# One core, forward and gradients of a two-branch block: the transpose of P by two DMAs of 16 blocks instead of one of 32, and a new order of all engines

## The chip, the cores and the metric

The kernel runs on one core of one Trainium2 chip. The metric is the device time of one execution in microseconds; lower is better. The kernel before took 1228.71 us in the median of three runs (1227.66 to 1231.55). One further execution was recorded with the hardware profiler; all rows of a profile in this document come from such a recorded execution, and their times count from its start.

A core has engines that run side by side, each through its own list of instructions in a fixed order: TensorE (PE, with its weight loads listed as PEld), VectorE (DVE), ScalarE (ACT), GpSimd (POOL) and SyncE (SP), which here issues transfers. An instruction waits, at the head of its list, until what it reads has been written and what it overwrites has been read. A transfer issued by SP is carried out by the DMA engines and lands later.

## The reference, cut to what matters

The reference is a block with two branches, run forward and then differentiated for a given `grad_out`. There are nine outputs: the block's output and the gradients of x and of seven weights. B = 2, T = 4000, D = 144, all bf16.

```
def _fwd_reference(x, w_qkv, w_att_out, w_mlp_in, dw_csgu, w_mlp_out, dw_merge, w_merge):
    xa = _layernorm(x, axis=-1)
    qkv = jnp.einsum('btd,de->bte', xa, w_qkv)
    ...
    scores = jnp.einsum('btd,bsd->bts', q, k) * D ** (-0.5)
    p = _softmax(scores, axis=-1)
    attn = jnp.einsum('bts,bsd->btd', p, v)
    glob = jnp.einsum('btd,de->bte', attn, w_att_out)
    ...
    loc = jnp.einsum('btd,de->bte', u * gc, w_mlp_out)
    m = jnp.concatenate([glob, loc], axis=-1)
    ...
    return x + jnp.einsum('btc,cd->btd', m, w_merge)

    _out, _vjp = jax.vjp(_f, x, w_qkv, w_att_out, w_mlp_in, dw_csgu, w_mlp_out, dw_merge, w_merge)
    _grads = _vjp(grad_out)
```

Most of the work is attention over 4000 positions and its gradient, which needs the 4000 x 4000 matrix of each batch several times.

## The kernel before, in words

The two batches follow each other. `phase_att` handles one batch in 32 tiles of 125 query positions (`PB`); a row of the score matrix is 32 blocks of 125 columns, stored 128 apart (4096 per row). A tile passes through several steps of one loop over `t`, so that a step works on several tiles at once:

- `products(q)`, q = 0 to 3: TensorE computes a chunk of 1000 columns of the scores S of tile t, and of dP (the gradient of the probabilities) of tile t−1. One chunk is four products of 500 columns and four remainders (L1059, L1065), called Q4 below.
- `S_min` (VectorE, L1083, L1085) copies a chunk of S into the buffer of P with the row minimum, `P_exp` (ScalarE, L1091) makes the exponentials in place, chunk by chunk in the order 1, 0, 3, 2.
- `P_tr` (L1095) transposes the whole row of P, 32 blocks, by one DMA that SP issues, from the buffer `Pb` into the one buffer `PT` (a part of `SX`). There are four buffers of P, three of S, and one `PT`.
- `Y_half` (L1115) reads `PT` in two halves of 16 products each and accumulates Y = P times the normalised x (with a column of ones for the row sum) in `yz`; called Y16 or Y32. VectorE then takes the reciprocal of the row sum (L1122) and the delta of the softmax gradient, ScalarE writes `yn` and `ty` (L1129, L1132), GpSimd the scaled rows that X needs (L1140 to L1144).
- `PdP` makes dS = dP times P: ScalarE casts a chunk of dP (L1104) and VectorE multiplies (L1106), or VectorE does both at once (L1101). `st_half` (L1287) transposes dS by two DMAs of 16 blocks each, and `Z_half` (L1162) multiplies them in two halves, called Z16. `zt_tr` (L1176) and the transposes of `qt` (L1041) and of `dhT` (L674) are further, smaller DMAs of the same queue.
- `X_group` (L1207) accumulates the gradient for the keys and values from untransposed P and dS; VectorE adds it up (L1213). The local branch is cut into small pieces that stand between these (L552 to L709).

Ahead of the loop stands a head: weights are multiplied together (L196 to L322), the first tiles of x are normalised and transposed (L459, L464), and 126 products that feed nothing (`WARM`, L154) keep TensorE running while data come in. Behind each batch come the weight gradients, the output and dx (L1487 to L1646), for the first batch beside the start of the second. In the very last tile of a batch the transposes are made on TensorE (`last_tr`, L1152), so 31 tiles of each batch use `P_tr`: 62 in all.

The order of every engine's instructions is written out by hand in the table `ORDER`: for each engine a list of numbers, each the difference to the one before, that name groups of instructions in the program's own order. `Planner.plan` turns the list into dependencies between neighbours, so an engine follows it exactly. What stands in the program decides only which data an instruction needs, and which numbers it has.

Of the kernel before, what the change touches and what calls it, by code (L numbers as in the profile page):

```python
# [747 lines left out]
for _s in """  # L748
PE 10 1 1 1 1 1 1 1 1 1 1 1 1 1 1 1 1 1 1 1 1 1 1 1 1 1 1 1 1 1 1 1 1 1 1 1 1 1 1 1 1 1 1 1 1 1 1 1 1 1 1 1 1 1 1 1 1 1 1 1 1 1 1 1 1 1 1 1 1 1 1 1 1
# [217 lines left out]
def phase_att(k, W, b, S, A, M, head=None, late=None, extra=None):  # L967
# [6 lines left out]
    with ExitStack() as es:  # L974
# [118 lines left out]
        def P_tr(i):  # L1093
            PL.tag("pt")
            nc.sync.dma_start_transpose(out=PT[:], in_=Pbuf[:, i % NPB, :])  # L1095
# [168 lines left out]
        for t in range(NB + 1):  # L1264
# [36 lines left out]
            if head is not None and t < 2:  # L1301
# [17 lines left out]
                if t == 0:  # L1319
                    P_tr(0)  # L1320
# [15 lines left out]
            pe(*((1,) if t < NB else range(4)))  # L1336
            products(0)
            pe(*((0,) if t < NB else ()))
            outs(2)
            if ok(t - 3):  # L1340
                zt_tr(t - 3)
            loc(0.25)
# [765 lines left out]
```

## Time and profile before

| | before |
|---|---|
| median of 3 runs | 1228.71 us |
| profiled execution, its own time | 1229.65 us |
| its span | 1227.9 us |
| mean granted TensorE clock | 0.996 |
| TensorE busy | 1183.7 us |
| VectorE busy | 1048.0 us |
| ScalarE busy | 734.7 us |
| GpSimd busy | 442.0 us |
| DMA queue of the transposes (q1), share of 16 engines | 86.4% |

A row of a group or of the timeline gives start, busy time, engine, line, operation, written and read tiles and, in brackets, how long the engine had been idle before it and for what. Engines ending in q (SPq) are the sequencers that issue transfers; the time of such a row is that of issuing. A row of a window gives from:to, its length, the busy time of PE, PEld, DVE, ACT and POOL, the granted clock, the DMA engines' mean busy share and GB/s. A row of the waits gives engine, line, what it waited for, us in total, times, and the longest. The rows themselves are shown in the prediction.

### The profile page before, as it was taken

To read this page: it belongs to the slowest core of one execution; us is meant where nothing else is said; L and a number is where in the kernel's file an instruction comes from. 1 tells how busy PE (TensorE), PEld (TensorE's weight loads), DVE (VectorE), ACT (ScalarE), POOL (GpSimd) and SP (SyncE) were. 2 spreads that over 40 slices of the span, in tenths; PEclk is the share of its full clock that TensorE was granted. 3 is DMA by queue.
4 is the path that set the end of the run, shared out by engine and by line. 5 is a ranking of instruction groups with operands and counts; after the bars stand their busy time and mean duration, and the time that the engine had idled before them with its cause. 6 is when DMAs were issued, how large, how long until landed. Compare 5 with 4: busy or idle time off the path is not lost.

```text
span 1227.9 us, 38426 instructions
## 1 busy us (share of the span) xinstructions
PE 1183.7 (96%) x15619; PEld 929.9 (76%) x15619; DVE 1048.0 (85%) x2856; ACT 734.7 (60%) x1303; POOL 442.0 (36%) x910
## 2 busy tenths in 40 slices
PE   9899999999999999998899999999999999998998
PEld 7567777777777777778777777777777777776987
DVE  7688989898989898878579998989898889996775
ACT  5866666666666666545747656666656565564461
POOL 8444334343443442314124433343433333332100
PEclk9999999999999999999899999999999999999999
DMA  3589899989999999997949899999899989999892
GB/s 107 111 147 159 149 175 161 166 148 166 164 149 169 154 166 169 150 200 147 180 102 167 157 161 169 163 165 164 141 172 160 171 155 168 162 163 173 161 167 69
DMA packets 681980, 191.81 MB, mean 156 GB/s; under 512 B 670572, under 2 KB 677481, under 8 KB 681796
## 3 DMA queue, kind: packets, MB, share of 16 engines
q1 hardware_dynamic: 656278, 181.97, 86.4%
q10 hardware_dynamic: 25348, 7.13, 3.0%
q8 instruction: 122, 2.00, 0.7%
q14 instruction: 56, 0.46, 0.1%
q0 software_dynamic: 176, 0.25, 0.1%
HBM read 20.44 MB, written 14.47 MB: 28 GB/s over the span
## 4 chain that ended last, share of the span: by engine, by line
PE 30%; DVE 11%; DMA 4%; ACT 2%; POOL 2%; issue 2%; SPq 1%; DVEq 0%; POOLq 0%; ACTq 0%
PE X L1207 7%; PE ps L1059 6%; PE yz L1115 3%; PE po L1609 3%; PE yz L1162 3%; DVE Pb L1083 3%; PE ps L1065 2%; DMA out_dram<-Pb 1%; DMA SX<-Pb 1%; DVE acc L1213 1%; DMA SX<-SX 1%; DVE SX L1101 1%; DVE SX L1106 1%; ACT Pb L1091 1%; PE po L1611 1%
## 5 line engine op out<-in xcount | busy, mean ns | idle before, releaser
L1091 ACT ACTIVATE Pb<-Pb,nm 125x1000 bf16<-125x1000 bf16 x256 | 273.7, 1124 | 127.0 <-DVE nm L1085 122.4
L1083 DVE TENSOR_SCALAR_CACHE_REDUCE Pb<-ps 125x1000 bf16<-125x1000 f32 x256 | 306.1, 1196 | 50.6 <-PE ps L1065 48.7
L1207 PE MATMUL X<-SX 125*128 125x144 bf16 x2048 | 293.0, 227 | 3.1 <-DVE acc L1213 1.7
L1207 PE MATMUL X<-SX,Pb 125*128 125x144 bf16 x2048 | 291.4, 226 | 2.8 <-DVE SX L1138 1.3
L1104 ACT CAST SX<-ps 125x1000 bf16<-125x1000 f32 x189 | 188.3, 996 | 142.3 <-PE ps L1065 136.7
L1059 PE MATMUL ps<-xaT_m,qt 128*128 128x500 bf16 x1024 | 261.3, 374 | 7.3 <-DVE Pb L1083 5.8
L1207 PEld LDWEIGHTS <-SX 125*128 125x128 bf16 x2048 | 197.3, 97 | 31.6 <-issue 31.0
L1213 DVE TENSOR_TENSOR acc<-X,acc 125x432 f32<-125x432 f32 (+1 forms) x372 | 199.4, 549 | 9.4 <-PE X L1207 8.8
L1207 PEld LDWEIGHTS <-Pb 125*128 125x128 bf16 x2048 | 200.2, 98 | 5.1 <-issue 4.1
L1162 PE MATMUL yz<-xa_aug,SX 125*128 125x144 bf16 x2048 | 149.7, 228 | 3.8 <-DMA SX<-SX 2.8
L1115 PE MATMUL yz<-xa_aug,SX 125*128 125x145 bf16 x2048 | 144.6, 228 | 5.7 <-DMA SX<-Pb 5.6
L1059 PEld LDWEIGHTS <-qt 128*128 128x128 bf16 x1024 | 91.8, 97 | 70.6 <-issue 12.3
L1106 DVE TENSOR_TENSOR SX<-SX,Pb 125x1024 bf16<-125x1024 bf16 x189 | 132.1, 702 | 9.1 <-ACT SX L1104 8.9
L1115 PEld LDWEIGHTS <-SX 125*128 125x128 bf16 x2048 | 133.6, 98 | 7.3 <-DMA SX<-Pb 7.0
L1162 PEld LDWEIGHTS <-SX 125*128 125x128 bf16 x2048 | 132.9, 98 | 8.1 <-DMA SX<-SX 4.3
L1065 PEld LDWEIGHTS <-qt 16*128 16x128 bf16 x1024 | 26.4, 91 | 109.7 <-issue 109.7
L1065 PE MATMUL ps<-XR,qt 16*128 16x500 bf16 x1024 | 102.7, 380 | 0.0
L1101 DVE TENSOR_TENSOR SX<-ps,Pb 125x1000 bf16<-125x1000 f32 x67 | 79.9, 1193 | 1.1 <-PE ps L1065 1.1
L557 POOL TENSOR_SCALAR l_a<-l_sq 125x576 bf16<-125x576 bf16 x32 | 23.3, 727 | 130.0 <-ACT l_sq L555 129.5
L1142 POOL TENSOR_SCALAR g<-qz,rl 125x144 f32<-125x144 bf16 x62 | 24.3, 393 | 116.3 <-DVE rl L1122 110.0
L662 POOL TENSOR_SCALAR l_w<-gdr,nc,c 125x144 f32<-125x144 bf16 x64 | 33.9, 534 | 59.7 <-DVE nc L658 32.5
L1487 PE MATMUL Hps<-Yg,go_h 125*128 125x144 bf16 x640 | 51.5, 228 | 0.3 <-DMA Yg<-Yn_d 0.3
(608 smaller groups left out, 2085.6 us busy)
## 6 DMA issues: line engine op xcount, KB each, us to landing
go_h<-in_grad_out_dram SPq DMA_DIRECT2D x4, 567.0 KB
Zn_d<-qz ACTq DMA_DIRECT2D x64, 35.2 KB
Yn_d<-yn ACTq DMA_DIRECT2D x64, 35.2 KB
ug_d<-ugr ACTq DMA_DIRECT2D x32, 70.3 KB
SX<-in_x_dram SPq DMA_DIRECT2D x16, 140.6 KB
out_dram<-Pb SPq DMA_DIRECT2D x16, 140.6 KB
out_dram<-SX SPq DMA_DIRECT2D x16, 140.6 KB
Pb<-in_grad_out_dram SPq DMA_DIRECT2D x8, 252.0 KB
```

The lines of the kernel that those rows point to most:

```text
L1059: mm = nc.tensor.matmul(pp[r // 2][:, r % 2, 0:CH], QT[i][:, 3 * h, :], xaTm[:, c * CH:(c + 1) * CH], start=True, stop=False)
L1065: nc.tensor.matmul(pp[r // 2][:, r % 2, 0:CH], QT[i][rs, 1 + h, :], xr, start=False, stop=True)
L1083: nc.vector.tensor_scalar(pv(Pbuf, i % NPB, c2), src, -1.0, 3.0e38, op0=ALU.mult, op1=ALU.min, accum_out=NM[i][:, c2:c2 + 1])
L1091: nc.scalar.activation(v, v, ACT.Exp, bias=NM[i][:, 4:5], scale=-1.0)
L1101: nc.vector.tensor_tensor(pv(Sbuf, i % NDB, c2), src, pv(Pbuf, i % NPB, c2), op=ALU.mult)
L1104: nc.scalar.copy(pv(Sbuf, i % NDB, c2), src)
L1106: nc.vector.tensor_tensor(sc, sc, pchunk(i % NPB, c2), op=ALU.mult)
L1115: nc.tensor.matmul(Y, PT[0:PB, j, :], xaa[:, j, 0:D + 1], start=(j == 0), stop=(j == NB - 1))
L1162: nc.tensor.matmul(Z, ST[0:PB, j, :], xaa[:, j, 0:D], start=(j == 0), stop=(j == NB - 1))
L1207: nc.tensor.matmul(X[:, jj, :], l, r, start=(n_ == 0), stop=(n_ == len(ops) - 1))
L1213: nc.vector.tensor_tensor(av, X[0:PB, 0:nj, :], av, op=ALU.add)
L1487: nc.tensor.matmul(H[a // 6][0:rows, a // 3 % 2, (a % 3) * D:(a % 3 + 1) * D], lhs, self.src[h][:, j, :], start=(j == 0 and a % 3 == 0), s ...
```

## The change

`P_tr` gets a second argument: half h of `PT` is transposed by a DMA of its own with 16 blocks. The first half (columns of chunks 0 and 1) is issued in the program right after the exponentials of chunks 1 and 0; the second half stands where the whole stood, after those of chunks 3 and 2. The first tile of a batch issues both halves together. No instruction is otherwise added or removed; the number of transposes of P rises from 62 to 124. The table `ORDER` is wholly new, for every engine (two of its rows are shown, cut).

```diff
 ORDER = {}
 for _s in """
-PE 10 1 1 1 1 1 1 1 1 1 1 1 1 1 1 1 1 1 1 1 1 1 1 1 1 1 1 1 1 1 1 1 1 1 1 1 1 1 1 1 1 1 1 1 1 1 1 1 1 1 1 1 1 1 1 1 1 1 1 1 1 1 1 1 1 1 1 1 1 1 1 1 1
...
+ 1 1 1 1 1 1 1 1 1 1 1 1 1 1 1 1 1 1 1 1 1 1 1 1 1 1 1 1 1 1 1 1 1 1 1 1 115 -114 117 -116 1 1 1 1 115 2 14 -130 1 1 1 1 1 1 149 2 -150 1 1 1 1 1 1
...
-        def P_tr(i):
-            PL.tag("pt")
-            nc.sync.dma_start_transpose(out=PT[:], in_=Pbuf[:, i % NPB, :])
+        def P_tr(i, h):
+            PL.tag("pt" if h else "pu")
+            a, w = h * NB // 2, NB // 2
+            nc.sync.dma_start_transpose(out=PT[:, a:a + w, :], in_=Pbuf[:, i % NPB, a * 128:(a + w) * 128])
...
                 if t == 0:
-                    P_tr(0)
+                    P_tr(0, 0)
+                    P_tr(0, 1)
                 continue
...
             products(0)
             pe(*((0,) if t < NB else ()))
+            if t < NB and ok(t - 1):
+                P_tr(t - 1, 0)
             outs(2)
...
             products(1)
             pe(*((3, 2) if t < NB else ()))
             if t < NB and ok(t - 1):
-                P_tr(t - 1)
+                P_tr(t - 1, 1)
```

The new function adds two lines, so the lines below it have moved: P's transpose is L1097 after, the exponentials L1092, the casts L1106, the transposes of dS L1289, `qt` L1042, `zt` L1178, `yn` L1131 and `ty` L1134.

Three places show how the table moves work. The rows are each engine's list, without times; a tile's name is followed by its shape, and x2 means twice in a row. First, SP in the middle of the first batch, at one step: `SX<-SX` is a half of dS, `SX<-Pb` is P. Before:

```order
L1287 DMA_TRANSPOSE SX<-SX 128x16x128
L1095 DMA_TRANSPOSE SX<-Pb 128x32x128
L1287 DMA_TRANSPOSE SX<-SX 128x16x128
L1041 DMA_TRANSPOSE qt<-qz 128x4x128
L674 DMA_TRANSPOSE dhT<-dhr_346 128x6x128
L1287 DMA_TRANSPOSE SX<-SX 128x16x128
```

After:

```order
L1289 DMA_TRANSPOSE SX<-SX 128x16x128
L1097 DMA_TRANSPOSE SX<-Pb 128x16x128
L1042 DMA_TRANSPOSE qt<-qz 128x4x128
L674 DMA_TRANSPOSE dhT<-dhr_346 128x6x128
L1097 DMA_TRANSPOSE SX<-Pb 128x16x128
L1289 DMA_TRANSPOSE SX<-SX 128x16x128
L1178 DMA_TRANSPOSE zt<-qz 128x2x128
L1289 DMA_TRANSPOSE SX<-SX 128x16x128
```

The first half stands where the whole stood, right behind a half of dS; `qt` and `dhT`, which followed the whole, are now between the two halves, and the half of dS that followed directly comes behind the second.

Second, ScalarE at the same tile (21 of the first batch), with the four exponentials (`Pb<-Pb,nm`). Before:

```order
L1104 CAST SX<-ps 125x8x125 x2
L1167 DMA Zn_d_78<-qz 125x144
L1091 ACTIVATE Pb<-Pb,nm 125x8x125 x3
L1129 ACTIVATE yn<-yz,rl 125x144
L1132 ACTIVATE ty<-yz,nd 125x144
L1091 ACTIVATE Pb<-Pb,nm 125x8x125
L1104 CAST SX<-ps 125x8x125
```

After:

```order
L1106 CAST SX<-ps 125x8x125 x2
L1092 ACTIVATE Pb<-Pb,nm 125x8x125
L1169 DMA Zn_d_78<-qz 125x144
L1092 ACTIVATE Pb<-Pb,nm 125x8x125
L1131 ACTIVATE yn<-yz,rl 125x144
L1134 ACTIVATE ty<-yz,nd 125x144
L1092 ACTIVATE Pb<-Pb,nm 125x8x125
L1106 CAST SX<-ps 125x8x125
L554 CAST l_hs<-ph 125x288
L555 ACTIVATE l_sq<-ph 125x288
L1026 CAST qz<-pj 125x2x144
L1092 ACTIVATE Pb<-Pb,nm 125x8x125
```

Three exponentials stood together and the fourth behind `yn` and `ty`; now they stand one or two together, and the last comes behind a cast of dP and three instructions of the local branch and of `qz`.

Third, SP at the end of the second batch, from the second-to-last tile (29) that uses `P_tr` to the last (30). Before:

```order
L1095 DMA_TRANSPOSE SX<-Pb 128x32x128
L108 DMA goT<-in_w_qkv_dram 16x432
L1041 DMA_TRANSPOSE qt<-qz 128x4x128
L1287 DMA_TRANSPOSE SX<-SX 128x16x128
L1176 DMA_TRANSPOSE zt<-qz 128x2x128
L1287 DMA_TRANSPOSE SX<-SX 128x16x128
L108 DMA goT<-in_w_att_out_dram 16x144
L1095 DMA_TRANSPOSE SX<-Pb 128x32x128
L674 DMA_TRANSPOSE dhT<-dhr_11900 128x6x128
```

After:

```order
L1097 DMA_TRANSPOSE SX<-Pb 128x16x128
L108 DMA goT<-in_w_att_out_dram 16x144
L1042 DMA_TRANSPOSE qt<-qz 128x4x128
L108 DMA goT<-in_w_qkv_dram 16x432
L1097 DMA_TRANSPOSE SX<-Pb 128x16x128
L1289 DMA_TRANSPOSE SX<-SX 128x16x128
L1178 DMA_TRANSPOSE zt<-qz 128x2x128
L1289 DMA_TRANSPOSE SX<-SX 128x16x128
L674 DMA_TRANSPOSE dhT<-dhr_11931 128x6x128
L1097 DMA_TRANSPOSE SX<-Pb 128x16x128 x2
```

Tile 29's halves have two small loads and `qt` between them; `dhT`, which followed the last P, now stands ahead of its two halves. On TensorE, Y of tile 29 is moved ahead of 20 products of X there, and Y of tile 30 behind 7 more of them. Two more moves on TensorE: of the 126 products that feed nothing, 92 stood ahead of the first transposes of x (L459), now 112; and between the groups of four products of L322, in the head, there now stands half a Z.

More of the change, by code (lines that the diff above doesn't have):

```diff
@@ L749 @@
 PE 10 1 1 1 1 1 1 1 1 1 1 1 1 1 1 1 1 1 1 1 1 1 1 1 1 1 1 1 1 1 1 1 1 1 1 1 1 1 1 1 1 1 1 1 1 1 1 1 1 1 1 1 1 1 1 1 1 1 1 1 1 1 1 1 1 1 1 1 1 1 1 1 1
[31 rows of a table removed]
-DVE 9 127 -128 165 20 1 5 -3 -1 5 -2 14 -15 18 -14 1 12 -72 114 4 -56 -1 59 -57 1 52 -48 3 80 -85 49 -48 46 4 -23 -25 31 -26 22 6 -4 -22 82 -1 -80 1 1
[48 rows of a table removed]
-Activation 148 1 -4 -1 2 5 -1 -3 94 -4 -13 1 2 1 2 16 1 107 -106 -16 1 1 37 -36 46 74 1 -80 1 8 -6 82 -52 14 -4 -5 1 47 -3 -1 -41 18 5 4 16 -3 -4 -4
[29 rows of a table removed]
-Pool 428 -265 19 261 -257 -2 -8 -39 48 -46 301 -300 302 2 -306 36 255 -252 30 -32 68 -4 -56 -40 36 43 -81 40 9 251 -249 -1 -3 1 94 4 149 -109 -58 23
[18 rows of a table removed]
-SP 0 1 2 -1 151 -146 -3 1 149 -148 149 14 -17 6 1 1 -3 9 4 -3 -2 6 -3 -7 -5 8 205 -1 137 1 1 1 2935 1 -3014 134 2 -33 -20 100 -53 1 -3 46 14 46 7 29
[12 rows of a table removed]
[31 rows of a table added]
+DVE 9 127 -128 165 20 1 5 -3 -1 5 -2 14 -15 18 -14 1 12 -72 114 4 -56 -1 59 -57 1 52 -48 3 80 -85 49 -48 46 4 -23 -25 31 -26 22 6 -4 -22 82 -1 -80 1 1
[48 rows of a table added]
+Activation 148 1 -4 -1 2 5 -1 -3 94 -4 -13 1 2 1 2 16 1 111 -126 129 1 -129 1 1 36 10 4 -9 1 79 -108 31 30 44 7 -41 -5 1 8 21 10 -19 5 17 -40 42 -10
[29 rows of a table added]
+Pool 428 -265 19 262 -258 -2 -8 -39 48 -46 302 -301 303 2 -307 36 255 -252 30 -32 68 -4 -56 -40 36 43 -81 40 9 252 -250 -1 -3 1 94 4 150 -168 38 -55
[18 rows of a table added]
+SP 0 1 2 -1 151 -146 -3 1 149 -148 149 14 -17 6 1 1 -3 9 4 -3 -2 6 -3 -7 -5 8 204 1 138 -1 2 2966 -2965 -78 -1 135 2 -53 20 81 -30 -24 -2 47 68 -112
[13 rows of a table added]
 """.strip().replace("\n ", " ").split("\n"):
```

277 rows, old and new, of the table ORDER are left out of this document.

## The prediction

> **What bounds the kernel now.** I read the page's busy line and groups first, then the windows, then the waits, and last the timeline where the waits lie.
>
> ```profile
> PE 1183.7 (96%) x15619; PEld 929.9 (76%) x15619; DVE 1048.0 (85%) x2856; ACT 734.7 (60%) x1303; POOL 442.0 (36%) x910
> 300.00:400.00 100.00, 99.33 (x1288) 75.62 (x1288) 92.57 (x243) 62.56 (x98) 40.66 (x81) 1.00 0.99 165
> L1115 PE MATMUL yz<-xa_aug,SX 125*128 125x145 bf16 x2048 | 144.6, 228 | 5.7 <-DMA SX<-Pb 5.6
> ```
>
> TensorE is busy 96% of the span, and in the middle of the first batch 99.3% of 100 us, with the DMA engines at 0.99 there too. So there is no stage in which a shorter path through the DMA could be worth much; what can be won on TensorE is the 4% in which it sits idle. The third row is the product that reads the transposed P (`Y_half`): over the whole kernel it waited 5.6 us for the transposes of P. That is the size of the target. The waits of the queue that issues the transposes are far larger:
>
> ```profile
> SPq L1095 <- ACT SX L1104: 168.8, 37, 7.8
> PE yz L1115 <- DMA SX<-Pb: 5.6, 5, 2.7
> ```
>
> The queue stood 168.8 us with P's transpose at its head until ScalarE had come past the exponentials, but TensorE noticed only five times. A transpose that can start after two chunks instead of four shortens a wait that is hidden in all but these five steps. The last of the five is the longest:
>
> ```profile
> 1106.56 4.19 ACT L1091 ACTIVATE Pb<-Pb,nm 125x1000 bf16<-125x1000 bf16 x4
> ...
> 1099.02 5.49 SPq L1095 DMA_TRANSPOSE SX<-Pb  x1
> ...
> 1114.38 5.43 SPq L1095 DMA_TRANSPOSE SX<-Pb  x1
> ...
> 1107.93 2.19 PE L1115 MATMUL yz<-xa_aug,SX 125*128 125x145 bf16 x32
> ...
> 1122.68 3.84 PE L1115 MATMUL yz<-xa_aug,SX 125*128 125x145 bf16 x32 [2.68 <-DMA SX<-Pb]
> ...
> 1125.00:1130.00 5.00, 5.00 (x59) 4.13 (x58) 2.95 (x8) 0.84 (x1) 3.00 (x8) 0.87 1.33 192
> ```
>
> The wait of 2.68 us is followed by 32 products that took 3.84 us where the step before took 2.19, at a granted clock of 0.87: another 1.65 us. So this one wait cost 2.68 + 1.65 = 4.33 us. Note also that the exponentials were over at 1106.56 + 4.19 = 1110.75, and the transpose began at 1114.38: here the queue itself was late, not ScalarE.
>
> **The change, part by part.**
>
> *One transpose of 32 blocks becomes two of 16.* The nearest rows are the whole transpose and the halves in which S is transposed already:
>
> ```profile
> L1095 SPq DMA_TRANSPOSE SX<-Pb x62: 4751/5282/7043, 40.0 to 1114.4; - x62
> ...
> 71.65 4.72 SPq L1287 DMA_TRANSPOSE SX<-SX  x2
> 403.47 5.87 SPq L1287 DMA_TRANSPOSE SX<-SX  x2
> ```
>
> Two halves back to back take 4.72 to 5.87 us on the queue, one whole 4.75 to 7.04. Bounds for 62 further issues are therefore −1 to +1 us each on the queue; I take 0, since the pairs lie in the lower part of the whole's range. The bytes are the same. If the DMA side did pay more, the cover is the slack below.
>
> *The last wait.* In the last step the transpose was issued at 1114.38 and landed when Y started, at 1122.68: 8.30 us, of which 5.43 issue and 2.87 landing. By halves: 2.1 us of issue (from the row of pairs) plus 2.87, so the first half lands some 5 us after its start and the second 8.3 as before. In the new order the queue holds, from the second-to-last P to the last, one `dhT` more (1.55 us at 1119.86 in the old place) and the second half of P(29), so the last pair starts at about 1114.3 again (1099.02 + two halves 4.2 + qt 1.68 + two small loads 1.1 + two S halves 4.28 + zt 1.67 + dhT 1.55 + ten gaps of 0.1 = 1114.5). Y's first 16 products no longer wait (landed at 1114.5 + 2.1 + 2.9 = 1119.5; TensorE was free at 1122.68 − 2.68 = 1120.0, and 7 more products of X now stand ahead); the second half lands at 1114.5 + 8.3 = 1122.8 and is wanted at 1120.4 + 1.1 = 1121.5, so 1.3 us would be left if TensorE came as early as before.
>
> ```profile
> 1119.86 1.55 SPq L674 DMA_TRANSPOSE dhT<-dhr  x1
> 1105.23 1.68 SPq L1041 DMA_TRANSPOSE qt<-qz  x1
> 1107.02 1.88 SPq L1287 DMA_TRANSPOSE SX<-SX  x1
> 1108.99 1.67 SPq L1176 DMA_TRANSPOSE zt<-qz  x1
> 1110.77 2.40 SPq L1287 DMA_TRANSPOSE SX<-SX  x1
> ```
>
> *A new wait one step earlier.* Products of X follow each other so, and the half of Z used below is the third row:
>
> ```profile
> 1113.09 0.23 PE L1207 MATMUL X<-SX 125*128 125x144 bf16 x1
> 1113.15 0.23 PE L1207 MATMUL X<-SX,Pb 125*128 125x144 bf16 x1
> ...
> 1115.03 1.18 PE L1162 MATMUL yz<-xa_aug,SX 125*128 125x144 bf16 x16
> ```
>
> For P(29) the new order puts two small loads and `qt` between the halves, and moves Y ahead of 20 products of X (20 at 0.06 us apart = 1.2 us). The second half starts at about 1099.02 + 2.1 + 0.53 + 1.68 + 0.53 + 0.4 = 1104.3 and lands at 1104.3 + 2.1 + 2.9 = 1109.3; it is wanted at 1107.93 − 1.2 + 1.1 = 1107.8. So TensorE waits 1.5 us here, and comes 1.5 us later to the last Y, whose second half is then in time. So the two waits give −4.0 (all but 0.3 of the 4.33) and +1.5; bounds 0 and −4.3 for the one, 0 and +2.8 for the other (2.8: the same two halves at 2.7 us each, half of the whole's 5.4).
>
> By the Trainium skill, "TensorE: Matmul & The Clock Gate", section on the HAM clock gate, the clock halves only after a whole idle window of about 3.4 us, which a wait of 2.68 us isn't; by that rule the 1.65 us would have another cause and stay, and this term would be −2.4. The trace shows a lowered clock right behind the wait (0.87 above), and I go by the trace.
>
> *The four other waits* come to 5.6 − 2.7 = 2.9 us. A first half that lands 3 us earlier ends the wait of the first 16 products, and the second half lands behind 1.1 us of them: −2.0, between 0 (the pair on the queue is issued no earlier) and −2.9.
>
> *TensorE's wait for GpSimd at 61 us.* Two of these products waited:
>
> ```profile
> 61.13 0.24 PE L322 MATMUL hps<-Pb,SX 128*128 128x144 bf16 x1 [1.18 <-POOL SX L316]
> 62.60 0.36 PE L322 MATMUL hps<-Pb,SX 128*128 128x144 bf16 x3 [1.23 <-POOL SX L316]
> ```
>
> The new order puts 16 products of Z (1.18 us) between their groups. One of the two waits is filled: −1.0 (0 to −2.4).
>
> *The head.* TensorE fills the time before the first tile with 126 products that feed nothing. Of these 92 stood ahead of the first transposes of x, now 112:
>
> ```profile
> 1.19 13.16 PE L154 MATMUL warm<-SX 128*125 128x290 bf16 x83 [1.19 <-DVE SX L151]
> 17.51 0.60 PE L459 MATMUL pt<-ident,xa_aug 125*128 125x125 bf16 x8
> 18.00:44.00 26.00, 23.10 (x225) 15.39 (x222) 18.82 (x50) 22.78 (x54) 18.45 (x56) 1.00 0.26 62
> ```
>
> 20 × 13.16/83 = 3.2 us later for the first transposes, and 20 fewer behind. From 18 to 44 us ScalarE is busy 22.78 of 26 us, so it can't catch up all of it, but TensorE (23.10, of which filler now leaves 3.2) can. I take +1.3, between 0 and +3.2.
>
> *Between the batches* TensorE loses 3 us behind an output store and the statistics of x:
>
> ```profile
> 591.24 0.76 DVE L1641 TENSOR_TENSOR Pb<-t,go_h 125x576 bf16<-125x576 f32 x1 [3.45 <-DMA out_dram<-Pb]
> 592.97 0.23 PE L459 MATMUL pt<-ident,xa_aug 125*128 125x125 bf16 x1 [1.55 <-DVE xa_aug L452]
> 594.87 1.14 PE L464 MATMUL pt<-ident,xa_aug 125*16 125x125 bf16 x8 [1.67 <-DVE acc L1213]
> 595.00:600.00 5.00, 5.00 (x45) 4.61 (x44) 3.04 (x13) 3.93 (x8) 0.00 (x0) 0.50 0.90 194
> ```
>
> The new table orders VectorE and the queue otherwise here, but the same store still stands ahead of the same statistics. I count 0; if the two waits of 3.2 us and the half clock behind them (5 us at 0.50, 2.5 us lost) went, −6; if another stall like one of these two with half a window of lowered clock came, +3.
>
> *The steps in between.* On the queue the first half stands behind the last half of S where the whole P stood, so nothing new is queued behind it: what it holds back was held back by the whole. The second half holds back the S halves and `zt` until the fourth exponential, as the whole did, but for half the issue time. On ScalarE the four exponentials (1.05 us each by 4.19/4) are spread in the new order: they lie within 4.8 rows of each other on average before, 7.4 now. So where they used to end together, the last now ends behind casts. The issue of a whole came 8.3 us (last pair above) or more before its Y; over the 62 pairs, of which these rows are the first, the distance is 10.6 in the median:
>
> ```profile
> 40.02 4.96 SPq L1095 DMA_TRANSPOSE SX<-Pb  x1
> 51.30 0.28 PE L1018 MATMUL pj<-XQ,XR 128*125 128x144 bf16 x1
> 51.85 2.19 PE L1115 MATMUL yz<-xa_aug,SX 125*128 125x145 bf16 x32
> L1104 ACT CAST SX<-ps 125x1000 bf16<-125x1000 f32 x189 | 188.3, 996 | 142.3 <-PE ps L1065 136.7
> ```
>
> So there are about 2 us of slack, and the second half is wanted 1.1 us later. Spreading by one cast of 996 ns is covered, by three isn't. I count 0.
>
> Sum: −4.0 + 1.5 − 2.0 − 1.0 + 1.3 + 0 = −4.2 us. Against the profiled execution's 1229.65 that is 1225.4; it lies 0.94 above the median of the three runs, so the median becomes **1224.5**.
>
> **The rivals.**
>
> *Hidden anyway* (0.25). TensorE at 99.3% and DMA at 0.99 say that most steps have nothing to gain, and each gain of 1 to 2 us can be taken back by the next wait: with the last wait merely moved to the second half (−1.5), the head at its upper end and half of the rest, the sum is −1.5 + 3.2 − 1.5 = 0: 1228.7. For it: only 5.6 us hang on P's transposes. Against it: the queue's 168.8 us show that half the issue can come earlier. [...]
>
> *The second half comes late* (0.35). This is the slower side. Its place is ScalarE: where a cast of dP or the local branch's pieces stand between the second and the fourth exponential, the second half is issued later than the whole was. It decides from 2 + 1.1 ≈ 3 us of delay, three casts at 1.0 us. About 20 of the 62 steps have their exponentials spread over 9 rows or more; if each of these lost 0.5 us on TensorE, that is +10, and with the gains of 4.2 about +6: 1235. For it: ScalarE's order has only a few us of room, as the 168.8 us of the queue's waits for it show. Against it: the same rows say that the queue used to wait for the end of a cast as well, and ScalarE is busy 60%.
>
> *The change doesn't start the first half earlier.* It needs Y's first 16 products of the tile before, since there is one buffer for the transposed P; in the trace Y ended at 1107.93 + 2.19 = 1110.12 while the exponentials of the next tile ran from 1106.56. Then the first half could start 0.6 us before the last exponential's end at most, and the time is that of *hidden anyway*.
>
> **How the numbers follow.** A measurement of this kernel tells about 0.3% (3.7 us) from no change. The likeliest case, 1224.5 (0.40, own range 1219 to 1228), lies just beyond that below 1225.0: faster 0.40. Hidden anyway 0.25, 1228.7, within 1225 and 1232.4. Late halves 0.35, 1235, up to 1242 if 30 steps lost 0.5 us. The range leaves out a tenth at each end: 1217 (all bounds of the gains without the transition, 1228.7 − 4.3 − 2.9 − 2.4 = 1219, and a third of the −6) to 1239.
>
> **What would show it.** Right: Y's wait for P's transposes falls from 5.6 to under 3 us, and the last Y takes 2.2 us for 32 products; the products at 61 us wait once; the first products of L1018 (at 51.30 above) come at about 52.6. Wrong: more waits of Y for the transposes, of many small ones (rival two), or other waits at the transition. A queue's wait for ScalarE still above 150 us would say that the first half isn't issued earlier. The prediction fails altogether if the new order opens a gap on TensorE in steady steps, which the window of 300 to 400 us would show at once.

## The result and the profile after

The changed kernel is slower: 1238.95 us in the median of six runs (1232.78 to 1241.62) against 1228.65 us before; the ratio is 1.007, with a 95% interval of 1.0051 to 1.0089. The forecast was 1224.5. The measured time lies at the very end of the stated range (1217 to 1239) and on the other side of no change. The profiled execution took 1235.81 us (span 1234.0), 6 us more than the one before. The ratios here and below leave out two executions far off the others, one of the kernel before (5127.7 us) and one of e11 (1437.71 us).

The first two lines are the busy times and the group of Y on the page of the kernel after; the rest are rows of its waits, with engine, line, what was waited for, us in total, times and the longest.

```profile
PE 1185.5 (96%) x15619; PEld 931.9 (76%) x15619; DVE 1048.5 (85%) x2856; ACT 740.2 (60%) x1303; POOL 437.4 (35%) x910
L1117 PE MATMUL yz<-xa_aug,SX 125*128 125x145 bf16 x2048 | 144.0, 227 | 7.5 <-DMA SX<-Pb 7.5
PE yz L1117 <- DMA SX<-Pb: 7.5, 9, 1.9
PE yz L1164 <- DMA SX<-SX: 3.6, 5, 2.0
PE fpt L1794 <- ACT Pb L1781: 3.0, 1, 3.0
PE hps L322 <- POOL SX L316: 0.4, 1, 0.4
SPq L1097 <- ACT SX L1106: 79.3, 40, 4.4
```

TensorE does the same work in nearly the same busy time (1183.7 us before). The queue's largest wait for ScalarE at a transpose of P fell from 168.8 to 79.3 us. That is one row of many, though: all waits at P's transposes together fell only from 302.2 us (300.0 ended by ScalarE, 2.2 by TensorE) to 244.7 us (205.6 and 39.1). Nor did a transfer get a longer lead over its reader: the one issued first starts 10.7 us ahead of its Y in the median of the 62 pairs, where the whole started 10.5 us ahead, and the one issued second starts 6.5 us ahead. Y's wait for P's transposes rose from 5.6 to 7.5 us instead of falling, and there is a wait of 3.0 us for weight products near the end (L1794). In the kernel before, the products of that line (L1789) waited so; the second row is that of the same products (behind the cast L1776, which is L1781 after):

```profile
PE fpt L1789 <- ACT Pb L1791: 1.1, 1, 1.1
...
PE fpt L1789 <- ACT Pb L1776: 0.3, 1, 0.3
```

Where the time went is read best from a product that every step has once, the first of `jit_mm` (L1018 before, L1019 after). These are its starts in the fifth, 29th, 35th and 61st of the 62 steps, before and then after:

```profile
108.10 0.23 PE L1018 MATMUL pj<-XQ,XR 128*125 128x144 bf16 x1
486.73 0.23 PE L1018 MATMUL pj<-XQ,XR 128*125 128x144 bf16 x1
665.67 0.28 PE L1018 MATMUL pj<-XQ,XR 128*125 128x144 bf16 x1
1080.09 0.23 PE L1018 MATMUL pj<-XQ,XR 128*125 128x144 bf16 x1
```

```profile
108.17 0.23 PE L1019 MATMUL pj<-XQ,XR 128*125 128x144 bf16 x1
490.88 0.22 PE L1019 MATMUL pj<-XQ,XR 128*125 128x144 bf16 x1
666.80 0.23 PE L1019 MATMUL pj<-XQ,XR 128*125 128x144 bf16 x1
1083.47 0.23 PE L1019 MATMUL pj<-XQ,XR 128*125 128x144 bf16 x1
```

The differences of these starts, and from the last to the end of the span, cut each profile in five stretches. The same was done for every experiment below; times are us:

| kernel | head | steps of batch 1 | between | steps of batch 2 | rest |
|---|---|---|---|---|---|
| before | 108.1 | 378.6 | 178.9 | 414.4 | 147.8 |
| after | 108.2 | 382.7 | 175.9 | 416.7 | 150.5 |
| after, second profile (e15) | 109.7 | 382.3 | 178.8 | 415.8 | 150.0 |
| e1 old order, halves | 109.3 | 378.5 | 176.1 | 415.4 | 150.2 |
| e2 new order, whole P | 112.0 | 407.4 | 176.5 | 425.2 | 154.5 |
| e3 new order in the steps | 113.9 | 382.4 | 178.2 | 415.9 | 152.1 |
| e4 new order at the ends | 107.7 | 379.1 | 175.6 | 417.0 | 151.6 |
| e5 old order at the end | 108.2 | 384.8 | 179.1 | 413.6 | 148.6 |
| e6 halves together | 109.9 | 384.8 | 182.4 | 422.5 | 149.6 |
| e7 new order between | 108.0 | 379.0 | 179.3 | 416.7 | 149.4 |
| e8 new order at the end | 108.1 | 378.9 | 178.2 | 418.0 | 153.3 |
| e9 after, filled | 109.7 | 382.8 | 178.4 | 417.0 | 146.3 |
| e10 before, filled | 108.4 | 378.7 | 177.0 | 413.3 | 147.9 |
| e11 before, unfilled | 107.7 | 378.7 | 175.8 | 415.0 | 149.6 |
| e12 e8, filled | 108.3 | 378.9 | 179.8 | 417.3 | 151.7 |
| e13 new order on the queue | 108.7 | 387.2 | 178.8 | 419.9 | 147.5 |
| e14 old order on the queue | 108.4 | 383.8 | 176.9 | 413.7 | 150.2 |

The steps of the first batch repeat within 0.6 us: 378.5 to 379.1 in all eight profiles with the old order there, whole or halves, and 382.3 to 382.8 in four of the five with the new order and its queue (384.8 in e5). The other stretches scatter by 2 to 6 us from profile to profile, so a single profile says less there. The steps of the second batch took 413.3 to 418.0 us in the eight profiles with the old order and 413.6 to 417.0 in the five with the new, so no difference is shown there.

### The profile page after: what moved, and what is told of

Read it like the earlier page. It is cut to its first block, busy times and chain, and to the rows that moved or that the text cites. A ratio compares the mean times of both kernels' runs of the same rounds, so it can differ in the third digit from the quotient of the medians.

```text
span 1234.0 us, 38593 instructions
## 1 busy us (share of the span) xinstructions
PE 1185.5 (96%) x15619; PEld 931.9 (76%) x15619; DVE 1048.5 (85%) x2856; ACT 740.2 (60%) x1303; POOL 437.4 (35%) x910
## 4 chain that ended last, share of the span: by engine, by line
PE 61%; DVE 16%; DMA 9%; POOL 5%; ACT 5%; issue 3%; SPq 2%; ACTq 0%; DVEq 0%; POOLq 0%
PE X L1209 15%; PE ps L1060 12%; PE yz L1117 7%; PE yz L1164 6%; PE ps L1066 5%; DVE Pb L1084 5%; PE po L1614 3%; DMA SX<-Pb 3%; DVE acc L1215 2%; DMA SX<-SX 2%; DVE SX L1108 2%; PE warm L154 1%; DMA out_dram<-Pb 1%; PE pw L707 1%; DVE SX L1103 1%
## 5 line engine op out<-in xcount | busy, mean ns | idle before, releaser
L1092 ACT ACTIVATE Pb<-Pb,nm 125x1000 bf16<-125x1000 bf16 x256 | 277.6, 1127 | 124.0 <-DVE nm L1086 121.6
L1106 ACT CAST SX<-ps 125x1000 bf16<-125x1000 f32 x189 | 188.1, 995 | 143.6 <-PE ps L1066 137.1
L1215 DVE TENSOR_TENSOR acc<-X,acc 125x432 f32<-125x432 f32 x372 | 199.3, 549 | 12.2 <-PE X L1209 11.4
L1117 PEld LDWEIGHTS <-SX 125*128 125x128 bf16 x2048 | 131.9, 98 | 10.5 <-DMA SX<-Pb 9.5
L1142 POOL TENSOR_SCALAR SX<-qz,rl 125x144 bf16<-125x144 bf16 x62 | 25.4, 410 | 112.2 <-DVE rl L1124 104.7
```

The costliest lines, as they stand in the source:

```text
L1092: nc.scalar.activation(v, v, ACT.Exp, bias=NM[i][:, 4:5], scale=-1.0)
L1106: nc.scalar.copy(pv(Sbuf, i % NDB, c2), src)
L1117: nc.tensor.matmul(Y, PT[0:PB, j, :], xaa[:, j, 0:D + 1], start=(j == 0), stop=(j == NB - 1))
L1215: nc.vector.tensor_tensor(av, X[0:PB, 0:nj, :], av, op=ALU.add)
```

## The experiments

In all of these the tables of order were put together from those of the two kernels: `ORDER` lists the same groups in both but for the added halves, and at many places the lists of an engine have run through the same groups, so one table can be continued by the other there. "Adjacent halves" means that the second half stands right behind the first on the queue.

**The split alone, and the order alone.** e1 has the changed program and the old order of every engine; on the queue it differs so:

```order
 L473 DMA go_r<-in_grad_out_dram 124x2x16
-L1095 DMA_TRANSPOSE SX<-Pb 128x32x128
-L1287 DMA_TRANSPOSE SX<-SX 128x16x128 x2
+L1097 DMA_TRANSPOSE SX<-Pb 128x16x128 x2
+L1289 DMA_TRANSPOSE SX<-SX 128x16x128 x2
 L324 DMA VA_d<-SX 128x1296
```

> The order of before for every engine; only the transpose of P is cut in two, both halves where the whole stood. Theory 1 (the loss comes from the new order at the two ends and between the batches, through idle TensorE and the half clock behind it): 1224 to 1229 us, so no slower than before, perhaps 2 to 4 us faster if the last wait of Y (2.7 us and the slow clock) ends earlier. Theory 2 (second halves come late because the exponentials are spread in steady steps): no slower either, since the exponentials stand as before. Theory 3 (62 more transfers cost time by themselves; on the queue a half takes 2.82 us in the median, a whole 5.28): slower, about 1235 to 1239.

Measured: 1232.05 us against 1230.79, ratio 1.0009 (0.9991 to 1.0028): no difference. Cutting the transposes costs nothing that can be measured, and by itself brings nothing. The Trainium skill, "DMA: Bandwidth & Descriptors", section "Rules for kernel authors", says so of two transfers to disjoint partition halves (don't bother, both go over the same DMA engines). Here each part covers all 128 partitions and the cut runs along the blocks, which that rule does not name; e1 shows the same for it. Theory 3 falls.

e2 is the reverse: the program of before, with the new order and the whole P at the place of the second half.

```diff
-        def P_tr(i, h):
-            PL.tag("pt" if h else "pu")
-            a, w = h * NB // 2, NB // 2
-            nc.sync.dma_start_transpose(out=PT[:, a:a + w, :], in_=Pbuf[:, i % NPB, a * 128:(a + w) * 128])
+        def P_tr(i):
+            PL.tag("pt")
+            nc.sync.dma_start_transpose(out=PT[:], in_=Pbuf[:, i % NPB, :])
```

> The new order for every engine, with one whole transpose of P at the place of the second half. Theory 1: about as slow as the changed kernel, 1236 to 1240. Theory 2: slower than the changed kernel, above 1242, since now all of P waits for the last exponential. Theory 3: back to 1228 or 1229.

Measured: 1280.84 us, ratio 1.0411 (1.0381 to 1.0441). The row of Y in its waits:

```profile
PE yz L1115 <- DMA SX<-Pb: 40.9, 25, 3.9
```

The new order is built on halves: with a whole P at the place of the second half Y waits 25 times. So the halves are worth 42 us in this order (ratio 1.041 against 1.007); but the order that they allow is no better than the old one with a whole P.

**Which stretch costs.** e3 has the new order in the steady steps alone, e4 everywhere else; both have halves (adjacent where the order is old). The edit is the table: the old lists to the fifth product of L1019, the new ones to the 29th, the old to the 35th, the new to the 59th and the old to the end, and the reverse.

> Halves; the new order only in the steady steps (tile 4 to 28 of the first batch, 3 to 27 of the second), the old order with adjacent halves in the head, between the batches and at the end. Theory 1: 1226 to 1231. Theory 2: 1235 to 1239, the whole loss. Theory 3: the whole loss too.

> The reverse: halves; the new order in the head, between the batches and at the end, the old order with adjacent halves in the steady steps. Theory 1: 1235 to 1240, the whole loss. Theory 2: 1226 to 1230. Theory 3: the whole loss.

Measured: e3 1239.56 us, ratio 1.0072 (1.0046 to 1.0098); e4 1237.03, ratio 1.0052 (1.0035 to 1.0069). Neither theory has the whole loss: each part by itself loses most of it, and the two together (1.007) lose no more than one of them. The table says what of it is certain: the steps of the first batch take 3.8 us longer in e3, as in the changed kernel, and as before in e4.

e8 has the new order only behind the 59th product, e7 only from the 29th to the 35th, and e5 is the changed kernel with the old order behind the 59th.

> The changed kernel, with the old order (and adjacent halves) only from the end of the second batch's steps on (last three tiles and everything behind them). If the tail of the new order costs what the two profiles show from the last products of L1018 to the end (131.1 us before, 135.1 after, of which 1.3 is a chunk that stands on the other side), 2.7 to 4 us come back: 1234 to 1236. If the tail has no part in it: 1239.

> The old order with adjacent halves everywhere, the new order only between the batches (tile 28 of the first to tile 3 of the second). The profiles show the changed kernel gaining 1.8 to 3 us there. If that holds: 1226 to 1229 with before at 1230, the fastest of all; if it is only one run's clock: the same as before.

> The old order with adjacent halves, the new order only in the last three tiles and behind them. If the tail costs by itself: 3 to 5 us slower than before. If the tail's loss is only a consequence of what came before it: the same as before.

Measured: e8 1239.15 us, ratio 1.0075 (1.0051 to 1.0099); e7 1232.94, ratio 1.0026 (1.0009 to 1.0043); e5 1236.33, ratio 1.0051 (1.0025 to 1.0077). The new tail, with the seam to the old order ahead of it, costs by itself, by 0.5 to 1%. The gain of 3 us between the batches that one profile seemed to show isn't there; e7 is slower by 0.1 to 0.4%. Taking the tail back from the changed kernel brings some 2 us, which its interval does not tell from nothing.

**What costs in the tail.** These are, of the kernel after, one row of the queue, TensorE's rows at the end of the attention and at the weight products L1794, two of VectorE and one of ScalarE, and three windows (from:to, length, then busy us of PE, PEld, DVE, ACT and POOL, the granted clock, the DMA share and GB/s):

```profile
1119.55 4.64 SPq L1097 DMA_TRANSPOSE SX<-Pb  x2
...
1124.04 1.19 PE L1117 MATMUL yz<-xa_aug,SX 125*128 125x145 bf16 x16 [0.57 <-DMA SX<-Pb]
1126.72 1.19 PE L1117 MATMUL yz<-xa_aug,SX 125*128 125x145 bf16 x16 [1.49 <-DMA SX<-Pb]
...
1143.56 1.19 PE L1164 MATMUL yz<-xa_aug,SX 125*128 125x144 bf16 x16 [2.01 <-DMA SX<-SX]
...
1184.10 0.76 DVE L1646 TENSOR_TENSOR Pb<-t,go_h 125x576 bf16<-125x576 f32 x1 [4.90 <-DMA out_dram<-Pb]
...
1188.95 2.14 DVE L1581 TENSOR_TENSOR A_H<-Hps,A_H 128x432 f32<-128x432 f32 x4
...
1190.97 1.37 ACT L1781 CAST Pb<-A_H 128x1440 bf16<-128x1440 f32 x1
...
1192.40 0.78 PE L1794 MATMUL fpt<-xaT_m,Pb 128*128 128x144 bf16 x5 [3.02 <-ACT Pb L1781]
...
1145.00:1150.00 5.00, 5.00 (x62) 5.00 (x61) 0.84 (x2) 2.36 (x3) 1.30 (x2) 0.69 0.64 140
...
1144.65:1148.06 3.41, 3.41 (x34) 3.41 (x32) 0.37 (x1) 1.17 (x2) 1.11 (x2) 0.50 0.59 149
1190.00:1195.00 5.00, 2.60 (x20) 2.14 (x21) 4.92 (x12) 3.88 (x10) 0.00 (x0) 0.74 0.77 170
```

The last Y, the target of the change, waits 0.57 + 1.49 us at full clock, where it waited 2.68 and then ran at a lowered clock. Against that gain of 2.3 us stand two waits. The last Z waits 2.01 us for the second half of dS, which had no such wait before. And in the new order VectorE stands 4.90 us before an addition for dx that overwrites a buffer still being stored (L1646); the sums of the weight gradient (`A_H`, L1581) stand behind it in its list, then ScalarE's cast of them (L1781), then TensorE (L1794), and TensorE has those products ahead of the output's products (L1614), most of which stood ahead of them before. Behind both waits the clock is lowered: in the second of the windows above, which begins as Z runs, it is 0.50, and it is 1.00 in the 3.4 us on either side.

The kernel before already had two such waits for stores ahead of its sums (L1576), 1.25 and 1.96 us, so the new part is 1.7 us on VectorE and the place of TensorE's products:

```profile
1178.25 0.76 DVE L1641 TENSOR_TENSOR Pb<-t,go_h 125x576 bf16<-125x576 f32 x1 [1.25 <-DMA out_dram<-Pb]
1182.20 0.76 DVE L1641 TENSOR_TENSOR Pb<-t,go_h 125x576 bf16<-125x576 f32 x1 [1.96 <-DMA out_dram<-Pb]
```

The chain is read from the lists and the waits; no run took the store away. The wait of Z does not come from the tail's new order alone: e3 and e5, which have the old order there, have it too (2.07 and 2.01 us), while e1 has none. In e5 the clock stays full behind it, and the rest of 148.6 us is about that of the kernel before (147.8).

e9 keeps the order of the changed kernel and gives TensorE work that feeds nothing at such places; e12 does the same at one place to e8.

```diff
-    keep_busy(k, W, 6, "ko")
+    keep_busy(k, W, 16, "ko")
...
+        if n == "xat1":
+            fill_yz(k, W, 26, "f_y")
```

The first two lines are the whole of e12. In e9 the products of `WARM` have their old places besides; `fill_yz` issues as many products of the identity with 290 columns as its number says, into an unused tile.

> The changed kernel with all orders kept, but TensorE kept at work with products that feed nothing: the 126 filler products of the head stand where they stood before, 26 products of 290 columns before the second transposes of x between the batches (the wait of 3.98 us), and 16 instead of 6 of 512 columns ahead of the last weight products (the wait of 3.02 us). Theory 1 (what the change loses, it loses to the half clock behind idle TensorE): the mean granted clock rises from 0.989 to 0.994 or more and the time falls by 5 to 8 us, to 1230 to 1234. Theory 2 (waits in steady steps): the clock rises, but the time stays at 1236 to 1240.

> The kernel of e8 (old order, adjacent halves; new order only in the last three tiles and behind them) with 16 instead of 6 filler products ahead of the last weight products, nothing else. If the new tail costs by the wait of TensorE there and the half clock behind it: 5 to 9 us faster than e8's 1239, at 1230 to 1234. If the wait is on the path and the clock only goes with it: 1237 to 1240.

Measured: e9 1233.16 us against 1230.5, ratio 1.0014 (0.9991 to 1.0037), so with idle TensorE filled most of the loss is gone, as theory 1 expected; its interval lies below that of the changed kernel, and the mean clock over its runs is 0.996 against 0.989. e12 1235.49 us, ratio 1.005 (1.0033 to 1.0067), against 1.0075 for e8: some 3 us, with intervals that overlap. These are the two rows of the weight products in e8 and in e12:

```profile
1194.49 0.78 PE L1794 MATMUL fpt<-xaT_m,Pb 128*128 128x144 bf16 x5 [5.71 <-ACT Pb L1781]
```

```profile
1193.82 0.49 PE L1794 MATMUL fpt<-xaT_m,Pb 128*128 128x144 bf16 x5 [2.64 <-ACT Pb L1781]
```

The ten more fillers stand in the place of idle time, and the products start only 0.7 us earlier, since they wait for ScalarE. Five of them take 0.49 us instead of 0.78, at a clock of 0.93 in 1190 to 1195 us against 0.60 in e8; in the next 5 us the clock is lowered in both (0.73 and 0.71). How the 3 us divide between clock and wait is not shown. In e9 the steps of the first batch are as long as in the changed kernel (382.8), and its rest is the shortest of all (146.3, one profile); which of the three fillers did it was not tried one by one.

The same was asked of the kernel before, with fillers added at its own two stretches of lowered clock (e10), and with most of its own fillers behind the head taken away (e11):

```diff
-    keep_busy(k, W, 9, "kx")
+    keep_busy(k, W, 16, "kx")
...
+        if n == "xat1":
+            fill_yz(k, W, 10, "f_y")
...
+            if b == 1 and i == NB - 2 and h == 0:
+                PL.tag("f_a")
+                for _ in range(34):
+                    nc.tensor.matmul(Y[0:PB], W.ident[:, 0:PB], W.VUT[:].rearrange("p a b -> p (a b)")[:, 0:D + 1], start=True, stop=True)
```

> The kernel before, with such fillers at the two places where its profile shows a half clock: between the batches (16 instead of 9 of 512 columns, and 10 of 290 columns ahead of the products that waited 1.67 us) and ahead of the last Y (34 of 145 columns, where it waited 2.68 us). Theory 1: clock 0.998, 1225 to 1227, faster than before by 3 to 5 us. If the half clock costs nothing because other engines set the time there: the same as before.

```diff
-    keep_busy(k, W, 9, "kx")
+    keep_busy(k, W, 1, "kx")
...
-    keep_busy(k, W, 6, "ko")
+    keep_busy(k, W, 1, "ko")
```

> The kernel before with its own fillers taken away (1 instead of 9 between the batches, 1 instead of 6 near the end): no order changed, no work added. Theory 1: the granted clock falls to 0.990 to 0.993 and the time rises by 2 to 6 us. Theory 2: the same as before, or faster by the 2 to 3 us that the fillers take on TensorE.

Measured: e10 1231.75 us, ratio 1.0012 (0.9993 to 1.0031), with a mean granted clock over its runs of 0.997 (before: 0.994); e11 1230.84, ratio 1.0002 (0.9979 to 1.0026), clock 0.993. Both expectations of theory 1 missed: filling raised the clock and won nothing, taking the fillers away cost nothing. That does not show that a lowered clock is free. The fillers of e10 also lengthen TensorE's busy time, from 1183.7 to 1186.2 us, and in e11 the clock over the runs hardly fell. And within one kernel clock and time go together: of 87 executions of the kernel before, run beside the experiments, the 25 with a mean clock of 0.992 or less took 1232.6 us in the median, the 17 with 0.997 or more 1227.7. Whether the lowered clock takes that time, or only shows the waits that do, was not separated. The place matters too: between the batches the changed kernel has waits of 3.27 and 3.98 us and a clock of 0.50 in 600 to 605 us, and that stretch is no longer than before (175.9 against 178.9), so other engines may set the time there; no run shows which.

**What costs in the steady steps.** e6 is the changed kernel with the second half moved up directly behind the first (and the first put ahead where it stood behind), here in the first steps:

```order
-L1097 DMA_TRANSPOSE SX<-Pb 128x16x128
+L1097 DMA_TRANSPOSE SX<-Pb 128x16x128 x2
 L473 DMA go_r<-in_grad_out_dram 124x2x16
 L1289 DMA_TRANSPOSE SX<-SX 128x16x128
 L1042 DMA_TRANSPOSE qt<-qz 128x4x128
-L1097 DMA_TRANSPOSE SX<-Pb 128x16x128
```

> The changed kernel, with the second half of P directly behind the first on the queue in every step; in the new order 39 of the 62 pairs have other transposes between them. If Y waits because the second half stands behind qt, zt or dhT on a queue that never rests, Y's waits for P (7.5 us) fall below 3 us and the time to 1234 to 1236. If Y waits because the last exponentials come late, the pair now holds up qt, zt and dhT for the same exponentials: no faster, 1238 to 1243.

Measured: 1250.99 us, ratio 1.0177 (1.0155 to 1.0199). The theory that separated halves are simply a mistake falls: moved up, the second half stands at the head of the queue until the last exponential and holds up what is behind it, and the waits move there:

```profile
PE yz L1164 <- DMA SX<-SX: 10.1, 10, 2.4
PE yz L1117 <- DMA SX<-Pb: 6.9, 7, 2.5
```

e13 and e14 divide the new order of the steady steps between the queue and the compute engines. e13 is e1 with the new list of the queue there, e14 is e3 with the old one.

> The old order on all compute engines; only the queue of the transposes has the new order in the steady steps (39 of the pairs separated by other transposes). Read from the profile: the time from the fifth to the 29th first product of L1019 is 378.5 to 379.1 us in every profile of the old order, 382.4 to 382.8 in three of the new. If the queue's order is what costs there: 382 or more. If the compute engines' order is: 378 to 379.5.

> The reverse: in the steady steps the new order on all compute engines, the old order (adjacent halves) on the queue. Same stretch: 378 to 379.5 if the queue's new order costs, 382 or more if the compute engines' order does; more than 390 if the new order of the compute engines needs the first half early, as e2 (a whole P: 407) suggests.

> The changed kernel once more, unaltered, for a second profile. If the steady steps of the first batch cost 4 us by the order, the same stretch is 382 to 383.5 again; if the first profile was chance, 378 to 380. The tail behind the last products (150.5 in the first profile, 147.8 before) tells how far the tail scatters.

Measured in the steps of the first batch, in one profile each: e13 387.2, e14 383.8, the changed kernel again 382.3. Both lists cost: the new queue under the old compute engines 8.6 us over the old order, the new compute engines with the old queue 5.2, the two together 3.7 to 4.1. Of e13's 8.6 us the one step shown below has some 6: a wait of 4.31 us, and 32 products in 3.84 us that take 2.19 at full clock. First two rows of e13 (all of Y's waits for P, and the longest), then rows of e14's waits in 108.2 to 490 us:

```profile
PE yz L1117 <- DMA SX<-Pb: 10.3, 7, 4.3
395.98 3.84 PE L1117 MATMUL yz<-xa_aug,SX 125*128 125x145 bf16 x32 [4.31 <-DMA SX<-Pb]
```

```profile
PE X L1209 <- POOL SX L1146: 1.6, 2, 0.9
PE ps L1060 <- DMA qt<-qz: 1.1, 1, 1.1
PE yz L1117 <- DMA SX<-Pb: 0.4, 1, 0.4
```

In e13 Y waits for halves that the queue issues late. In e14 Y hardly waits, but the products of X wait for GpSimd's scaled rows and the scores for `qt`. In the changed kernel the first two are there; the same stretch of its waits:

```profile
PE X L1209 <- POOL SX L1146: 1.7, 3, 0.9
PE yz L1117 <- DMA SX<-Pb: 1.7, 3, 1.0
```

The kernel before, in the same stretch, has this row for X and none for Y:

```profile
PE X L1207 <- POOL SX L1144: 0.3, 1, 0.3
```

Y's 1.7 us and X's 1.4 us more are 3.1 of the 4.1 us that the steps lost; for the last us the rows name no wait. One of the three waits of Y, with the queue, ScalarE and TensorE of the kernel after:

```profile
412.15 1.24 SPq L674 DMA_TRANSPOSE dhT<-dhr  x1
413.56 2.88 SPq L1097 DMA_TRANSPOSE SX<-Pb  x1
416.53 1.72 SPq L1042 DMA_TRANSPOSE qt<-qz  x1
418.30 1.24 SPq L1178 DMA_TRANSPOSE zt<-qz  x1
419.59 2.71 SPq L1097 DMA_TRANSPOSE SX<-Pb  x1
...
410.81 1.12 ACT L1092 ACTIVATE Pb<-Pb,nm 125x1000 bf16<-125x1000 bf16 x1
...
425.50 1.19 PE L1117 MATMUL yz<-xa_aug,SX 125*128 125x145 bf16 x16 [0.46 <-DMA SX<-Pb]
```

The last exponential ended at 411.93, before even the first of the two transfers was issued at 413.56. The second came 7.7 us after that end because `qt` and `zt` stood between the two and the queue was hardly idle from 412 to 427 us.

The half that Y needs first is not always issued first. By the numbers in `ORDER` the queue issues the second half (chunks 3 and 2) ahead of the first in 15 of the 62 pairs. Tile 23, shown here, is one of them, and so is tile 21, shown under the change: what stands there in the place of the whole is its second half. In these steps Y's first 16 products wait, by the semaphores in the trace, for the transfer issued second. Five of the nine waits of Y, 3.6 of the 7.5 us, lie in such steps; in three the last 16 products wait for the second half, and in one the first 16 for the first half. The longest wait of e13 is that of tile 21: the first transfer starts at 381.28 us, and the half that Y reads first at 389.55, behind `qt` and `dhT`. No run turned these 15 pairs alone. In 30 pairs other transfers stand between the halves; the 39 of the expectations include 9 that are side by side the other way round.

No kernel here beat the one before.

## Why the prediction was wrong, point by point

- **The sum counted the steps in between at nothing; that is the step that failed first.** "Spreading by one cast of 996 ns is covered, by three isn't. I count 0." The new order costs 3.7 to 4.2 us in the steps of the first batch in four profiles of five (6.2 in e5), and by itself too (e3). In the second batch no difference is shown. The rival *second half comes late*, with a chance of 0.35, came nearest in the number (1235), but partly by luck: it looked for the delay in the spread exponentials on ScalarE, which were not tried by themselves. At tile 23 the delay lay in the transposes between the halves on the queue, and in 15 pairs in their being issued the other way round; beside it stand waits of X for GpSimd (1.4 us more) that no part of the prediction spoke of. Its size, 0.5 us in 20 steps, was too large: Y waits for P three times in the steps of the first batch, 1.7 us in all.
- **"The four other waits" (−2.0) had the wrong sign.** Before they came to 2.9 us, after to 7.5 − 2.06 = 5.4. The prediction took an early landing of the first half and let the second land as before. But the transfer issued first starts no earlier against Y than the whole did (10.7 us ahead, 10.5 before), the second 4 us later, and in 15 pairs it is the second that Y reads first. The remark that the first transfer needs the one buffer free bore out in part: TensorE ended 39.1 us of the queue's waits at P's transposes, 2.2 before.
- **The last wait and the new one (−4.0 and +1.5) came out at −2.3**, 0.2 from their sum. That is luck: both halves of tile 30 wait (0.57 and 1.49 us) and tile 29 doesn't, where the working had it nearly the other way round. The clock stays up: 4.33 us became 2.06.
- **The tail behind the last Y had no term at all.** The prediction weighed the new table at the places that the changed instruction touches. The table also reorders VectorE, ScalarE, the stores and TensorE in the last 100 us, and there the profile has a new wait of 2.01 us and one of 3.02 that was 0.3, with a lowered clock behind each. e8 shows that this tail alone costs 0.5 to 1%; which of its waits does it is read from the profile and was not tried one by one.
- **GpSimd at 61 us (−1.0)**: the two waits of 2.4 became one of 0.4, so −2.0; but nothing of it is left by the fifth step (108.10 before, 108.17 after).
- **The head (+1.3)**: the first product of L1019 came 2.5 us later, at 53.76 against 51.30, for another reason too: the clock was lowered behind three waits. By the fifth step that was gone as well.

```profile
40.92 0.60 PE L411 MATMUL pt<-ident,Pb 125*128 125x125 bf16 x8 [0.79 <-ACT goT L417]
43.13 0.34 PE L1252 MATMUL pj<-VUT,goT 128*125 128x144 bf16 x2 [0.48 <-POOL goT L418]
44.44 0.28 PE L1257 MATMUL pt<-ident,qz 128*128 128x128 bf16 x2 [0.97 <-ACT qz L1036]
53.76 0.28 PE L1019 MATMUL pj<-XQ,XR 128*125 128x144 bf16 x1
45.00:50.00 5.00, 5.00 (x60) 2.58 (x59) 2.62 (x3) 3.72 (x9) 0.00 (x0) 0.56 0.55 105
```

- **Between the batches (0)**: right as far as the profiles tell, 175.6 to 179.8 us with either order but in e6 (182.4); by its runs e7, with the new order there alone, is 0.1 to 0.4% slower.
- **62 more transfers (0)**: right (e1), although a half takes longer to issue than half a whole: 2.82 us in the median, against 5.28 for the whole. The 2.1 us that the working takes for a half "from the row of pairs" is too little even by that row, whose halves are 2.36 and 2.94.

The loss does not add up. Some 4 us in the first batch's steps are shown by five profiles of the new order against eight of the old. The tail's part is not pinned down: e8 loses 6 to 12 us by its runs, its profile shows 5.5 us in the rest (153.3 against 147.8), and taking the tail back in e5 brings 2 us that are not told from nothing. That e3, e4 and e8 each lose 0.5 to 0.75% while all together lose 0.7% was not explained; each mixed table has seams of its own, and the runs of e3, for one, go from 1235.0 us at a mean clock of 0.997 to 1244.7 at 0.989.

## What to carry to other kernels

An early start of a transfer helps only the wait that it ends: before it is bought with a new order, add up that wait (here 5.6 us of 1229) and compare it with the room that the old order leaves everywhere else. On a queue that hardly rests, the second part of a transfer cut in two is late by whatever is put between the parts, whether its data are ready or not (7.7 us at tile 23); and which part the reader needs first has to be looked up, not assumed. And where a change brings a whole new table of order, the stretches that it does not mention must be costed too: the order of the last 150 us here has little to do with the transpose and costs 0.5 to 1% by itself.

## What the runs showed that was not expected

- The granted clock fell after short waits: 0.56 in 45 to 50 us, behind three waits of 0.79, 0.48 and 0.97 us, and 0.69 in 1145 to 1150 us behind one of 2.01. The Trainium skill, "TensorE: Matmul & The Clock Gate", section on the HAM clock gate, gives an idle window of about 3.4 us as the condition; here no single wait was that long, so the measurement differs from that rule, or a window need not be wholly idle. The length of the wait alone does not decide it either: the same Z waited 2.04 us in e8, and there the clock stayed at 1.00 (1144 to 1150 us).
- A higher mean clock bought with fillers was not a shorter time: 0.997 against 0.994 with the same time (e10). Between executions of one unchanged kernel it was: 1227.7 us at 0.997 or more, 1232.6 at 0.992 or less.
- The new order with a whole P costs 4% (e2). Cutting the 62 transfers in two is worth nothing in the old order (e1) and 42 us in the new one.
